# Packed attention and a channel mixer on one core: two loads placed later in the text, and the second batch's attention spread over 39 places of the first batch's loop

## The chip, the core and the metric

The kernel runs on 1 core of one Trainium2 chip. The metric is the device time of one execution in microseconds, so less is better. A core has five instruction queues that run beside each other and wait for one another through semaphores: TensorE (PE, matrix products), VectorE (DVE), ScalarE (ACT), GpSimd (POOL) and SyncE (SP, which issues the DMA transfers here). The profile lists TensorE's loading of stationary operands as a row of its own (PEld). Instructions on one queue run in the order in which the program put them there.

## The reference

There are 8 batches, 8 heads, 576 tokens, a head size of 64 and 32 "packing" queries per head. Attention runs twice, and its result goes through a token mixer of rank 32 and a channel mixer:

```python
p_packed = sm_attn(p, k, v)                  # 32 packed rows for each head
x = sm_attn(q, p_packed, p_packed)           # every token attends to those 32 rows
x = x.transpose(0, 2, 1, 3).reshape(B, S, H * D)
u = x + (x.transpose(0, 2, 1) @ U @ V).transpose(0, 2, 1)
out = u + maximum(u @ w_ch1, 0.0) @ w_ch2    # 512 -> 2048 -> 512
```

q, k, v and p are float32; U, V and both weights arrive as float64, read as pairs of 32-bit words, and are turned into float32 on the chip. `sm_attn` is a softmax over scaled scores.

## The kernel before

**Two stages.** In the first stage (up to about 121 us in the trace) 16 units, two for each batch, compute the packed rows, and the first batch's second attention is computed beside them. A scheduler orders this stage: it takes the text as given and places instructions by its own estimate of time. From line 552 on (`manual_schedule`) instructions stand on their queues in the order in which the code is written.

**The second stage.** For each batch b a loop of 16 steps kt does two products. `gemm1(kt)` makes a 128-wide slice of the hidden layer (12 TensorE products for lines 86 to 88, in two halves of 320 and 256 tokens); ScalarE takes its positive part (`hh`, `hj`), and VectorE the rest that the rounding left (`hl`, line 607). `gemm2(kt - 1)` multiplies the slice of the step before by a 128-row slice of w2, in four token tiles of three products each. Every value is carried as a high and a low part, hence three products for each.

**w2 is converted on the way.** In batch 0, step kt splits slice kt+1 into its parts (ScalarE `w2h`, line 158, GpSimd `w2l`, line 159), loads slice kt+3, and converts slice kt+2 from its 64-bit form: one ScalarE operation (line 77) and four VectorE operations in a row (lines 78 to 81). I call those four **a conversion**. Later batches have none of this.

**Folds.** At kt = 2, 6, 10, 14 `fold` multiplies the packed rows into w1 for the steps that come next: 16 products on TensorE (line 368) into two PSUM banks, and then four pairs of ScalarE `wth` (line 374) and VectorE `wtl` (line 375) that empty the banks.

**Attention in steps.** `attention(b)` returns 24 small steps for the batch after the one in the loop: `load`, then 23 others. By the names that the text uses: tq00 to tq02 and tq10 to tq12 turn the queries of head group 0 and 1 (lines 219 and 229, TensorE, then ScalarE copies, lines 226 and 230); sc0 and sc1 are the scores (line 240, TensorE, then VectorE lines 272 and 273); m0 and m1 subtract the maximum (VectorE line 278, GpSimd line 279); exp is line 282; s0 and s1 divide by the sum (VectorE lines 287 to 289, GpSimd line 290); aT0 and aT1 transpose back (VectorE line 294); tok0, tok2, tok4 (lines 247 and 249, then ScalarE line 308 and VectorE line 309), mix1 (line 316) and four v steps (lines 328 to 331) mix tokens. tq11 carries group 0's exp.

**Where steps may go.** A step kt has two places, A behind gemm1 and B behind gemm2 and the conversion (at the four fold steps the fold takes B). Four leftovers of the first stage (`rest`) sit in the middle of gemm2 of kt = 1 to 4, between its second and third tile; I call that place C. Empty entries in the list keep a place free.

**The two shared banks.** Folds, leftovers, and the steps that use TensorE all draw from one pool `psT` of two PSUM banks, in turns (`bank()`, tiles `t_ps`). A bank goes to the next user when ScalarE or VectorE has read it.

## Time and profile before

| What | Value |
| --- | --- |
| Median of 3 runs | 869.55 us (869.44 to 871.65) |
| Profiled execution, own time | 869.67 us |
| Its span, first to last instruction | 867.1 us |
| TensorE busy | 829.0 us (96%) |
| VectorE busy | 391.6 us (45%) |
| ScalarE busy | 330.2 us (38%) |
| GpSimd busy | 99.3 us (11%) |
| Batch 0's loop, first product of gemm1 of kt 0 to that of batch 1 | 121.13 to 217.09 us |

The profiled execution's own time is 2.57 us above its span and 0.12 us above the median. In rows of the timeline the first number is the start in us, the second the length in us; "x4" merges four instructions; a bracket gives the engine's idle time before the row and what ended it. In a list of waits the three numbers are the sum in us, the number of waits and the longest. A window's row has the length, and then for each engine the busy time and the number of instructions.

### The profile page before, as it was taken

Reading aid. Unit: us, or ns where it says so; the run is one execution under the profiler, and the core shown is the slowest. Engines: PE = TensorE matmul, PEld = TensorE weight load, DVE = VectorE, ACT = ScalarE, POOL = GpSimd, SP = SyncE. Lnnn points to the kernel's source line nnn. Section 1 sums busy time; section 2 is a strip of 40 time slices with the busy share of each in tenths; the row PEclk is TensorE's granted clock in tenths of the full one; section 3 lists DMA queues with packets and bytes.
Section 4 is the critical chain, followed back from the end, with each engine's and each line's share of the span. In section 5 each row is a group of like instructions: output and inputs, shape, how many; then the busy total and the mean of one; then the engine's idle time right before and its main releaser. Section 6 shows DMA issues by size and latency. Waiting matters only on the chain.

```text
span 867.1 us, 14707 instructions
## 1 busy us (share of the span) xinstructions
PE 829.0 (96%) x5792; PEld 659.4 (76%) x5792; DVE 391.6 (45%) x968; ACT 330.2 (38%) x1028; POOL 99.3 (11%) x128
## 2 busy tenths in 40 slices
PE   5879898989999999999999999999999999999997
PEld 2545566768888888788878878888888887888886
DVE  4689857797434423433343433434344234332221
ACT  3657664444432333234323333234323332342221
POOL 0002232333001100100010000110011001010000
PEclk8789999999999999999999999999999999999999
DMA  8999842332100110011001100011001100010001
GB/s 275 276 319 295 277 150 81 104 98 86 50 1 1 61 55 8 1 61 49 2 1 61 49 13 2 1 61 50 1 1 61 53 9 1 1 50 1 1 1 61
DMA packets 38981, 59.09 MB, mean 68 GB/s; under 512 B 11776, under 2 KB 21888, under 8 KB 38912
## 3 DMA queue, kind: packets, MB, share of 16 engines
q1 hardware_dynamic: 38912, 58.16, 21.1%
q8 instruction: 45, 0.74, 0.4%
q14 instruction: 24, 0.20, 0.1%
HBM read 47.79 MB, written 10.35 MB: 67 GB/s over the span
## 4 chain that ended last, share of the span: by engine, by line
PE 82%; DVE 8%; DMA 6%; ACT 2%; issue 1%; SPq 0%; POOL 0%; DVEq 0%; ACTq 0%
PE o L86 16%; PE o L88 16%; PE o L87 15%; PE h_ps L86 8%; PE h_ps L88 7%; PE h_ps L87 7%; PE t_ps L368 4%; DMA bits<-in_moe_w_ch_dram 2%; PE t_ps L219 2%; DVE os L80 1%; PE t_ps L240 1%; DVE os L78 1%; DMA kx<-in_k_dram 1%; PE s_ps L240 1%; PE t_ps L247 1%
## 5 line engine op out<-in xcount | busy, mean ns | idle before, releaser
L86 PE MATMUL o<-w2h,hh 128*128 128x512 f32 x512 | 206.4, 403 | 0.0
L88 PE MATMUL o<-w2h,hl 128*128 128x512 f32 x512 | 202.7, 396 | 0.0
L87 PE MATMUL o<-w2l,hh 128*128 128x512 f32 x512 | 202.3, 395 | 0.0
L607 DVE SCALAR_TENSOR_TENSOR hl<-h_ps,hh 128x256 fp32r<-128x256 f32 x256 | 104.3, 422 | 201.1 <-ACT hj L606 188.7
L604 ACT ACTIVATE hh<-h_ps 128x256 fp32r<-128x256 f32 x256 | 98.8, 388 | 181.2 <-PE h_ps L88 180.4
L86 PE MATMUL h_ps<-ah,wth 128*128 128x320 f32 (+1 forms) x512 | 158.0, 309 | 2.1 <-DVE hl L607 2.1
L87 PE MATMUL h_ps<-al,wth 128*128 128x320 f32 (+1 forms) x512 | 151.8, 296 | 0.0
L88 PE MATMUL h_ps<-ah,wtl 128*128 128x320 f32 (+1 forms) x512 | 151.6, 296 | 0.0
L86 PEld LDWEIGHTS h_ps<-ah,wth 128*128 128x128 f32 x512 | 96.9, 189 | 35.9 <-issue 27.0
L88 PEld LDWEIGHTS o<-w2h,hl 128*128 128x128 f32 x512 | 96.6, 189 | 22.8
L86 PEld LDWEIGHTS o<-w2h,hh 128*128 128x128 f32 x512 | 96.9, 189 | 20.0 <-issue 3.1
L87 PEld LDWEIGHTS o<-w2l,hh 128*128 128x128 f32 x512 | 96.9, 189 | 17.0
L87 PEld LDWEIGHTS h_ps<-al,wth 128*128 128x128 f32 x512 | 96.9, 189 | 1.7
L88 PEld LDWEIGHTS h_ps<-ah,wtl 128*128 128x128 f32 x512 | 97.1, 190 | 0.0
L375 DVE TENSOR_TENSOR wtl<-t_ps,wth 128x256 fp32r<-128x256 f32 x128 | 48.5, 420 | 92.5 <-ACT wth L374 89.1
L374 ACT CAST wth<-t_ps 128x256 fp32r<-128x256 f32 x128 | 43.5, 374 | 110.0 <-PE t_ps L368 95.7
L331 POOL TENSOR_TENSOR al<-aT,ah 128x320 fp32r<-128x320 f32 (+1 forms) x32 | 26.7, 836 | 206.5 <-ACT ah L330 206.5
L279 POOL TENSOR_TENSOR e<-e,m 128x576 f32<-128x576 f32 x16 | 19.7, 1229 | 236.6 <-DVE m L278 236.6
L368 PE MATMUL t_ps<-w1t,ppT 64*32 64x512 f32 x512 | 38.1, 601 | 0.3 <-DVE eT L455 0.2
L226 ACT COPY xT<-t_ps 128x256 f32<-128x256 f32 x60 | 20.4, 395 | 38.8 <-PE t_ps L219 38.2
L330 ACT CAST ah<-aT 128x320 fp32r<-128x320 f32 (+1 forms) x32 | 13.8, 434 | 46.5 <-DVE aT L329 46.5
L290 POOL TENSOR_TENSOR e<-e,s 128x576 f32<-128x576 f32 x16 | 18.6, 1160 | 106.2 <-DVE s L289 103.6
(130 smaller groups left out, 1009.6 us busy)
## 6 DMA issues: line engine op xcount, KB each, us to landing
bits<-in_moe_w_ch_dram SPq DMA_DIRECT2D x32, 512.0 KB, 4.8
kx<-in_k_dram SPq DMA_DIRECT2D x16, 576.0 KB, 6.5
x<-in_q_dram SPq DMA_DIRECT2D x16, 576.0 KB, 4.7
vt<-in_v_dram SPq DMA_DIRECT2D x64, 128.0 KB, 4.6
out_dram<-bits SPq DMA_DIRECT2D x32, 256.0 KB, 2.4
pn<-in_p_dram SPq DMA_DIRECT2D x16, 64.0 KB, 6.1
vt<-in_v_dram SPq DMA_DIRECT2D x16, 64.0 KB, 3.8
out_dram<-os SPq DMA_DIRECT2D x8, 128.0 KB, 2.3
```

Of the source, the lines that this page charges most:

```text
L86: nc.tensor.matmul(ps, lhsT=lh, rhs=rh, start=start, stop=False)
L87: nc.tensor.matmul(ps, lhsT=lh, rhs=rl, start=False, stop=False)
L88: nc.tensor.matmul(ps, lhsT=ll, rhs=rh, start=False, stop=stop)
L226: nc.scalar.copy(dst, src[:, a])
L279: nc.gpsimd.tensor_tensor(e, e, m.unsqueeze(2).to_broadcast([P, S // 32, 32]), op=ALU.subtract)
L290: nc.gpsimd.tensor_tensor(e, e, s.unsqueeze(2).to_broadcast([P, S // 32, 32]), op=ALU.mult)
L331: nc.gpsimd.tensor_tensor(al[:, g, ns], aT[:, ns], ah[:, g, ns].bitcast(F32), op=ALU.subtract)
L368: nc.tensor.matmul(f_ps[g][xs], lhsT=ppT[b][zs, g, xs], rhs=w1t[h // 2][zs, QW * c:QW * c + QW], start=True, stop=True)
L374: nc.scalar.copy(hi[:, g], f_ps[g][:, cs])
L375: nc.vector.tensor_tensor(lo[:, g], f_ps[g][:, cs], hi[:, g].bitcast(F32), op=ALU.subtract)
L604: nc.scalar.activation(hh[:, ms], src, AF.Relu)
L607: nc.vector.scalar_tensor_tensor(hl[:, ms], src, 0.0, hh[:, ms].bitcast(F32), op0=ALU.max, op1=ALU.subtract)
```

## The change

1. In the first stage the text puts the loads of w2's first two pieces and of batch 1's queries one or two units later (from units 12 and 13 to unit 14).
2. Batch 1's attention, spread over batch 0's loop, may now use C at every kt from 1 to 15 (the leftovers still take the first four). That makes 39 places, and the list of 23 steps gets 15 empty entries instead of 4; four of them come first.
3. Batch 2's `load` moves from kt 13 to kt 15 of batch 0. In batch 1 kt 0 holds no step, and place A at kt 2, 6, 10, 14 may hold one, so that batch 1's steps start one kt later and end one kt earlier. From batch 2 on nothing is changed.

```diff
-        if i == 12:
+        if i == 13:
+            fold(0, 0)
+        if i == 14:
             load_w2(0)
             load_w2(1)
-        if i == 13:
-            fold(0, 0)
             steps = attention(1, res)
             steps.pop(0)()
-        if i == 14:
             split_w2(*convert_w2(0))
             load_w2(2)
...
-    for n in (16, 15, 15, 12):
-        steps.insert(n - 1, lambda: None)
+    for n in (20, 19, 18, 15, 15, 14, 13, 12, 12, 11, 5, 0, 0, 0, 0):
+        steps.insert(n, lambda: None)
...
-            if steps and (b == 0 or kt % 4 != 2):
+            if steps and (b < 2 or kt % 4 != 2) and (b, kt) != (1, 0):
                 steps.pop(0)()
...
-                cur.gemm2(kt - 1, rest.pop(0) if rest else None)
+                cur.gemm2(kt - 1, (rest or steps).pop(0) if b == 0 and (rest or steps) else None)
...
-            elif steps:
+            elif steps and (b, kt) != (1, 0):
                 steps.pop(0)()
...
-            if ahead and kt == 13:
+            if ahead and kt == (13 if b else NK - 1):
                 ahead.pop(0)()
```

Popping both lists gives these places in batch 0 ("-" is empty; leftovers in C of kt 1 to 4 and folds in B are the same in both):

| kt | before A, B | after A, C, B |
| --- | --- | --- |
| 0 | tq00, tq01 | -, none, - |
| 1 | tq02, sc0 | -, leftover, - |
| 2 | m0, fold | tq00, leftover, fold |
| 3 | tq10, tq11 | tq01, leftover, tq02 |
| 4 | tq12, s0 | sc0, leftover, m0 |
| 5 | aT0, sc1 | -, tq10, tq11 |
| 6 | -, fold | tq12, s0, fold |
| 7 | m1, exp1 | aT0, sc1, - |
| 8 | s1, - | m1, -, - |
| 9 | -, aT1 | exp1, -, s1 |
| 10 | -, fold | -, aT1, fold |
| 11 | tok0, tok2 | -, -, tok0 |
| 12 | tok4, mix1 | tok2, tok4, - |
| 13 | v00, v10 | mix1, -, v00 |
| 14 | v01, fold | -, v10, fold |
| 15 | v11 | v01, v11 |

On the queues the first part leaves no trace: SP's queue has the same 118 rows with the same waits in both kernels, and the other queues are alike up to the first gemm1 of batch 0. What moves is in the loops of batch 0 and batch 1.

VectorE around kt 2 of batch 0, before: the end of slice 3's conversion (L80, L81), sc0's two rows (L272, L273), the residual's blocks, gemm1's `hl`, m0 (L278), a leftover (L455 to L458).

```order
L80 SCALAR_TENSOR_TENSOR os<-bits,os 128x512
L81 SCALAR_TENSOR_TENSOR os<-bits,os 128x512
L272 STREAM_TRANSPOSE e<-t_ps 128x320
L273 STREAM_TRANSPOSE e<-t_ps 128x256
L586 TENSOR_TENSOR rdl_1880<-ppall,rdh_1878 32x64 x8
L589 CAST ajl_1884<-al 128x2x64
L607 SCALAR_TENSOR_TENSOR hl<-h_ps_2061,hh 128x256
L607 SCALAR_TENSOR_TENSOR hl<-h_ps_2071,hh 128x256
L278 TENSOR_REDUCE m<-e 128x18
L455 COPY eT<-t_ps 64x128
L457 SCALAR_TENSOR_TENSOR rs<-sm 128x1
L458 RECIPROCAL rs<-rs 128x1
```

The same place of the changed kernel, whose line numbers are one lower from here on:

```order
L80 SCALAR_TENSOR_TENSOR os<-bits,os 128x512
L81 SCALAR_TENSOR_TENSOR os<-bits,os 128x512
L585 TENSOR_TENSOR rdl_1880<-ppall,rdh_1878 32x64 x8
L588 CAST ajl_1884<-al 128x2x64
L606 SCALAR_TENSOR_TENSOR hl<-h_ps_2029,hh 128x256
L606 SCALAR_TENSOR_TENSOR hl<-h_ps_2039,hh 128x256
L455 COPY eT<-t_ps 64x128
L457 SCALAR_TENSOR_TENSOR rs<-sm 128x1
L458 RECIPROCAL rs<-rs 128x1
```

sc0's and m0's three rows are gone from ahead of the leftover and of the conversion and the `wtl` rows that come next.

VectorE from kt 6 to kt 7 of batch 0 in the changed kernel: s0's last two rows, slice 8's conversion, the fold's `wtl`, `hl` of kt 7, aT0 (L294), sc1 (L272, L273).

```order
L288 TENSOR_SCALAR s<-s 128x18
L289 RECIPROCAL s<-s 128x18
L78 TENSOR_SCALAR os<-os 128x512
L79 TENSOR_SCALAR os<-os 128x512
L80 SCALAR_TENSOR_TENSOR os<-bits,os 128x512
L81 SCALAR_TENSOR_TENSOR os<-bits,os 128x512
L375 TENSOR_TENSOR wtl<-t_ps,wth 128x256 x4
L606 SCALAR_TENSOR_TENSOR hl<-h_ps_2430,hh 128x256
L606 SCALAR_TENSOR_TENSOR hl<-h_ps_2440,hh 128x256
L294 STREAM_TRANSPOSE aT_2449<-e 128x576
L272 STREAM_TRANSPOSE e<-t_ps 128x320
L273 STREAM_TRANSPOSE e<-t_ps 128x256
```

Before, s0, aT0 and sc1 were done by the end of kt 5, and neither s0's rows nor those of sc1 stood next to this fold.

TensorE at kt 12 of batch 0 in the changed kernel: tok2 (L247), the first two tiles of gemm2, tok4 (L249).

```order
L247 MATMUL t_ps<-ident,aT_2449 128x128
L247 MATMUL t_ps<-ident,aT_2611 128x128
L86 MATMUL o<-w2h_2310,hh 128x512
L87 MATMUL o<-w2l_2311,hh 128x512
L88 MATMUL o<-w2h_2310,hl 128x512
L249 MATMUL t_ps<-ident,aT_2449 64x128
L249 MATMUL t_ps<-ident,aT_2611 64x128
```

Here each kind of row stands once (four L247 and two tiles of three rows are in the queue). tok2 and tok4 are half a gemm2 apart now, and tok0 and tok2 a gemm1; before, tok0 and tok2 had a whole gemm2 between them, and tok2 and tok4 a gemm1.

## The prediction, made before the result was known

> **What bounds the kernel now.** I read the page's busy times first (in the table above), then the windows, then the list of waits inside batch 0, and last the timeline around each wait.

> ```profile
> 120.00:210.00 90.00, 82.74 (x629) 66.31 (x625) 68.76 (x131) 43.24 (x123) 27.22 (x31) 1.00 0.30 95
> 208.00:300.00 92.00, 91.63 (x588) 73.89 (x586) 36.51 (x91) 33.43 (x108) 11.29 (x13) 1.00 0.07 27
> ```

> TensorE sets the time. From batch 1 on it is hardly idle (0.37 of 92 us in the last row), so nothing is to be had there. Batch 0 leaves 7.26 us of 90 idle, and only there is VectorE close to full (68.76 of 90). The first stage is idle too, but its queues and waits are the same in both kernels. So the question is batch 0's loop, with batch 1's for a possible loss. Batch 0's waits, the three largest sorts of five:

> ```profile
> PE t_ps L219 <- DVE wtl L375: 2.7, 1, 2.7
> PE h_ps L86 <- DVE hl L607: 2.1, 3, 1.2
> PE t_ps L247 <- DVE wtl L375: 2.0, 1, 2.0
> ```

> These are 6.8 of the 7.26 us, and all three wait for VectorE. Recorded idle time is too small a measure, since the modelled tail of a product covers the start of a wait. I count instead from one start to the next. Here are the waits in order of place:

> ```profile
> 122.83 0.60 PE L219 MATMUL t_ps<-ident,x 128*128 128x128 f32 x4
> 123.60 0.66 PE L219 MATMUL t_ps<-ident,x 128*128 128x128 f32 x4 [0.17 <-ACT ppTa L481]
> 124.46 0.42 PE L86 MATMUL h_ps<-ah,wth 128*128 128x320 f32 x1 [0.21 <-DVE hl L607]
> ...
> 136.17 1.06 PE L368 MATMUL t_ps<-w1t,ppT 64*32 64x512 f32 x8
> ...
> 138.45 0.41 PE L86 MATMUL h_ps<-ah,wth 128*128 128x320 f32 x1
> ...
> 143.04 0.63 PE L219 MATMUL t_ps<-ident,x 128*128 128x128 f32 x4 [2.72 <-DVE wtl L375]
> 143.42 0.48 PE L86 MATMUL o<-w2h,hh 128*128 128x512 f32 x1
> ...
> 176.16 0.42 PE L86 MATMUL h_ps<-ah,wth 128*128 128x320 f32 x1 [0.74 <-DVE hl L607]
> ...
> 182.00 0.41 PE L86 MATMUL h_ps<-ah,wth 128*128 128x320 f32 x1 [1.19 <-DVE hl L607]
> ...
> 186.60 1.09 PE L368 MATMUL t_ps<-w1t,ppT 64*32 64x512 f32 x16
> 187.62 0.41 PE L86 MATMUL h_ps<-ah,wth 128*128 128x320 f32 x1
> ...
> 191.47 0.63 PE L247 MATMUL t_ps<-ident,aT 128*128 128x128 f32 x4 [2.00 <-DVE wtl L375]
> ...
> 210.28 2.22 PE L368 MATMUL t_ps<-w1t,ppT 64*32 64x512 f32 x16
> 212.43 0.41 PE L86 MATMUL h_ps<-ah,wth 128*128 128x320 f32 x1
> ```

> A turn (L219 x4) takes 0.38 (143.04 to 143.42), so kt 0 with two turns in 1.63 loses 0.9. A fold without a wait takes 1.02 (186.60 to 187.62); that of kt 2 takes 2.28, losing 1.26, and that of kt 14 takes 2.15, losing 1.13. The four large brackets are each short by about 0.17 of tail: 2.9, 0.9, 1.35, 2.15. **Sum before: 10.6 us.**

> **The change part by part.** *The two loads*: on the queues nothing moves, so 0. If a semaphore that the listing doesn't show differed, the first stage could shift by one load; the recorded waits for w1's and w2's bits there were the one kind touched, and I hold that at nothing. *Batch 2's load behind kt 15*: its two rows keep their place on SP, where they wait for mix1, and batch 2's queries are first used a whole gemm1 and gemm2 after kt 15. Nothing is queued behind them but the next packed rows and the first stores, with some 10 us to spare: 0.

> *The empty places at kt 0.* gemm1(1) needs VectorE's `hl`, which hangs on ScalarE:

> ```profile
> 123.28 0.27 ACT L481 COPY ppTa<-t_ps 128x128 f32<-128x128 f32 x1 [1.07 <-DMA ppTd<-ppTa]
> ...
> 123.98 0.76 DVE L607 SCALAR_TENSOR_TENSOR hl<-h_ps,hh 128x256 fp32r<-128x256 f32 x2 [3.20 <-ACT hj L606]
> ```

> ScalarE waits there for a transfer of the first stage, so gemm1(1) starts at 124.46 in either kernel. The two turns that filled part of that time now come later. The wait is the whole 122.83 to 124.46, **1.63** in place of 0.9.

> *kt 2 and 3.* VectorE before, and a plain conversion and a crowded one for comparison (first row to the row behind it):

> ```profile
> 133.49 0.51 DVE L272 STREAM_TRANSPOSE e<-t_ps 128x320 f32<-128x320 f32 x1
> ...
> 134.25 1.41 DVE L586 TENSOR_TENSOR rdl<-ppall,rdh 32x64 fp32r<-32x64 f32 x8
> ...
> 136.47 0.74 DVE L278 TENSOR_REDUCE m<-e 128x18 f32<-128x576 f32 x1
> 137.13 0.27 DVE L455 COPY eT<-t_ps 64x128 f32<-64x128 f32 x1
> ...
> 137.59 1.21 DVE L78 TENSOR_SCALAR os<-os 128x512 f32<-128x512 f32 x1
> ...
> 141.61 1.61 DVE L375 TENSOR_TENSOR wtl<-t_ps,wth 128x256 fp32r<-128x256 f32 x4
> ...
> 165.81 0.97 DVE L78 TENSOR_SCALAR os<-os 128x512 f32<-128x512 f32 x1
> ...
> 168.68 0.42 DVE L375 TENSOR_TENSOR wtl<-t_ps,wth 128x256 fp32r<-128x256 f32 x1
> ...
> 177.75 1.16 POOL L290 TENSOR_TENSOR e<-e,s 128x576 f32<-128x576 f32 x1 [3.26 <-DVE s L289]
> 178.87 1.47 POOL L159 TENSOR_TENSOR w2l<-os,w2h 128x512 fp32r<-128x512 f32 x1
> ...
> 176.35 0.74 DVE L287 TENSOR_REDUCE s<-e 128x18 f32<-128x576 f32 x1
> ...
> 177.52 0.36 DVE L78 TENSOR_SCALAR os<-os 128x512 f32<-128x512 f32 x1
> 177.92 1.28 DVE L79 TENSOR_SCALAR os<-os 128x512 int32<-128x512 int32 x1
> 179.23 1.66 DVE L80 SCALAR_TENSOR_TENSOR os<-bits,os 128x512 int32<-128x512 int32 x1
> ...
> 181.53 0.75 DVE L607 SCALAR_TENSOR_TENSOR hl<-h_ps,hh 128x256 fp32r<-128x256 f32 x2
> ```

> A conversion beside one GpSimd operation takes 2.87 (165.81 to 168.68). Beside two, w2l and a softmax operation, it takes 4.01 (177.52 to 181.53), or 4.02 (137.59 to 141.61). At kt 2 sc0 (0.76, 133.49 to 134.25) and m0 (0.66, 136.47 to 137.13) leave VectorE, and m0's GpSimd operation leaves with them, another 1.15. So `wtl` starts 2.57 earlier, at 139.0, and the fold no longer waits. TensorE arrives earlier too: sc0 (0.69 and two changes of 0.1) and tq02 (0.2) are gone, tq00 (0.45) has come, the fold's 1.26 is saved: gemm1(3) ends at 138.4 where it ended at 140.15. The bank comes back 1.43 after the first `wtl` starts (143.04 less 141.61), at 140.4. tq01 waits **1.95**, where tq10 waited 2.9, and the fold 0 for 1.26.

> *kt 4 to 6.* sc0 and m0 now stand beside one plain conversion each and no fold; adding up the rows, each `hl` is ready 1 us or more ahead of its use. No wait.

> *kt 6 and 7.* The walk brings `hl` of kt 6 to its end at 162.4 and TensorE to the fold at 163.4. s0's three rows take 1.17 (176.35 to 177.52) and stand directly ahead of slice 8's conversion, as s1 did at 177.5, so this takes 4.0. `wtl` starts near 167.5. The first bank is back 1.43 later, the second one `wtl` (0.4) after it, at 169.3. TensorE does the fold (1.1), gemm1(7) (1.7, as in 121.13 to 122.83) and two tiles of gemm2 (1.4, from 259.06 to 260.54 below, less a change) and asks for both banks for sc1 at 167.7. **1.6**. With a plain conversion it would be 0.5.

> [...]

> *kt 8 to 10.* The 0.9 and 1.35 before came of two crowded conversions in a row, with m1 and s1 at kt 7 and 8. Now m1 crowds one conversion only, and s1 stands behind one, with two empty places ahead. Each `hl` is ready 1 us or more ahead: **0**.

> *kt 11 and 12.* aT1 (0.7) goes ahead of one more conversion, but the whole gemm2 lies between the fold's `wtl` and tok0: **0.1** where it was 2.15. tok4 in place C of kt 12 needs tok0's bank, whose VectorE row stands behind a conversion that ends at 195.1: TensorE asks at 194.5 and gets it at 195.9, **1.3**.

> *kt 13 to 15.* v10 moves half a gemm2 ahead of the fold, which then finds both banks read: **0** for 1.13.

> **Sum after: 1.63 + 1.95 + 1.6 + 0.1 + 1.3 = 6.6**, 4.0 less than before. *Batch 1* gives some back: sc0 now comes directly behind a fold at kt 3, as sc1 does at kt 7 already:

> ```profile
> 257.67 0.28 PE L88 MATMUL h_ps<-ah,wtl 128*128 128x256 f32 x1
> 258.03 1.09 PE L240 MATMUL t_ps<-xT,ppT 64*32 64x320 f32 x16
> 259.06 0.50 PE L86 MATMUL o<-w2h,hh 128*128 128x512 f32 x1
> ...
> 260.54 0.39 PE L86 MATMUL o<-w2h,hh 128*128 128x512 f32 x1
> ```

> That takes 1.27 (257.79 to 259.06) for 0.8, so 0.4 lost. Two turns that stood together now stand apart, one more change of 0.1. Net gain 3.5: **869.67 - 3.5 = 866.2 us** for the profiled execution, and the median differs from that by 0.12.

> The unknown costs are the three new waits for a bank. Below, each could be nothing where VectorE runs a conversion earlier than my walk (then 4.85 more is gained); above, each could be as long as the longest wait for a bank in the trace, 2.9 (then 3.85 is lost). I take the walk's values, since each is a sum of recorded lengths, and walking the kernel before in this way came out within about 1 us at the end of batch 0.

> **Rivals.** *The waits only move.* VectorE's work in batch 0 is the same, and 68.76 of 90 us is already mean load with bursts. If sc1 waits 2.0, tok0 1.0, tok4 1.3 and the fold of kt 14 still 1.1 beside kt 0 and kt 3, the sum is 9.0, and with batch 1's 0.5 the gain is 1.1: 868.6. For it speaks that three of the waits were folds, and that folds stay. Against it, that the crowded conversions go from four to two or three.

> *Almost all waits go.* If the conversions behind m1 and s0 lose nothing, sc1 waits 0.5 and tok4 0.3: sum 4.5, gain 5.6, 864.1. Against it stands 4.01 at the same pattern.

> *Slower.* A wait in place C stops TensorE in the middle of gemm2, and five steps sit in C with a bank to take (tq10, sc1, tok4, v10, v11). If each waits 2.4 (the mean of 2.72 and 2.00), the sum is 12 + 1.63 + 1.95 = 15.6, 5.0 more than before, with batch 1 875.1. It decides from 1.4 each. Against it: tq10 takes a bank that ScalarE empties, and v10 and v11 come when conversions have ended.

> **How the numbers follow.** Forecast 0.55, waits only move 0.25, almost all go 0.14, slower 0.06. The range goes from 864.5 (short of the third) to 869.3 (past the second). A measurement of this kernel can tell about 0.3% or 2.6 us from no change, that is a time below 866.9. Of the forecast's 0.55 I put 0.46 beyond that: faster 0.60, same 0.34, slower 0.06.

> **What would show it.** Right: TensorE starts gemm1(1) at 124.46 with 1.6 us of wait; tq01 waits about 2 us for `wtl` at 140; sc1 and tok4 wait in the middle of gemm2; the two `hl` waits of 176 and 182 are gone; the windows from batch 2 on are as before. Wrong: a first stage that ends at another time, new waits for `hl`, a wait at tq10 or the v steps, or batch 1 longer by over 1 us.

## The result and the profile after

The changed kernel takes 866.91 us (median of 22 executions; 863.66 to 872.33), the kernel before 871.0 us on the same chip (22 executions). The ratio is **0.9949, with a 95% interval of [0.9931, 0.9968]**: 4.4 us less, between 2.8 and 6.0. A second comparison of the same two kernels gave 0.9963 [0.9941, 0.9985]. The forecast was 866.2 us.

The profiled execution of the changed kernel has a span of 862.9 us and an own time of 865.46 us, 4.21 less than before. Split by place, the first stage ends 0.99 earlier (the first product of gemm1(0) starts at 120.14 in place of 121.13), batch 0's loop takes 92.81 in place of 95.96, batch 1's 85.88 in place of 85.90, and the rest 564.09 in place of 564.15. So nearly all that the change itself did lies in batch 0, 3.15 us, of which 0.19 is a shorter kt 0.

The windows of the changed kernel that answer to the two shown of before, and one over the later batches, behind which the last row is that of the kernel before (length, then busy time and number of instructions of PE, PEld, DVE, ACT and POOL, then TensorE's granted clock and the transfers):

```profile
120.00:210.00 90.00, 84.16 (x619) 67.63 (x619) 69.02 (x135) 46.12 (x132) 28.24 (x28) 1.00 0.29 93
208.00:300.00 92.00, 91.67 (x583) 75.93 (x584) 37.06 (x93) 33.26 (x109) 11.39 (x14) 1.00 0.08 27
300.00:860.00 560.00, 556.90 (x3441) 459.32 (x3440) 197.13 (x490) 181.50 (x580) 42.19 (x50) 1.00 0.07 25
300.00:860.00 560.00, 558.63 (x3451) 461.45 (x3452) 200.41 (x498) 182.87 (x586) 42.88 (x51) 1.00 0.07 25
```

TensorE's idle time in the first row fell from 7.26 to 5.84 us. The row of batch 1 has 0.33 idle, where it had 0.37. Over the later batches the changed kernel's row has 1.73 us less of TensorE's work and ten products fewer, but no wait is recorded there in either kernel and the rest takes as long as before (564.09 for 564.15), so I take the later batches as unchanged. The list of TensorE's waits in batch 0, complete:

```profile
PE t_ps L240 <- DVE wtl L375: 1.7, 1, 1.7
PE t_ps L219 <- DVE wtl L375: 1.7, 1, 1.7
PE h_ps L86 <- DVE hl L606: 1.3, 1, 1.3
PE t_ps L249 <- DVE x L309: 0.8, 1, 0.8
PE t_ps L247 <- DVE wtl L375: 0.2, 1, 0.2
```

Before, the list was led by 2.7 at tq10, 2.1 in three waits for `hl`, and 2.0 at tok0. Now it is sc1 (L240), tq01 (L219), `hl` of kt 0, tok4 (L249) and a rest of tok0's. No wait is as long as 2 us. TensorE's timeline at those places:

```profile
123.28 0.42 PE L86 MATMUL h_ps<-ah,wth 128*128 128x320 f32 x1 [1.28 <-DVE hl L606]
...
134.30 1.45 PE L368 MATMUL t_ps<-w1t,ppT 64*32 64x512 f32 x16
135.68 0.42 PE L86 MATMUL h_ps<-ah,wth 128*128 128x320 f32 x1
...
139.24 0.63 PE L219 MATMUL t_ps<-ident,x 128*128 128x128 f32 x4 [1.70 <-DVE wtl L375]
...
165.39 0.40 PE L86 MATMUL o<-w2h,hh 128*128 128x512 f32 x1
167.99 1.09 PE L240 MATMUL t_ps<-xT,ppT 64*32 64x320 f32 x16 [1.74 <-DVE wtl L375]
169.01 0.50 PE L86 MATMUL o<-w2h,hh 128*128 128x512 f32 x1
...
188.58 0.40 PE L86 MATMUL o<-w2h,hh 128*128 128x512 f32 x1
189.61 0.63 PE L247 MATMUL t_ps<-ident,aT 128*128 128x128 f32 x4 [0.16 <-DVE wtl L375]
190.25 0.42 PE L86 MATMUL h_ps<-ah,wth 128*128 128x320 f32 x1
...
193.11 0.39 PE L86 MATMUL o<-w2h,hh 128*128 128x512 f32 x1
194.81 0.41 PE L249 MATMUL t_ps<-ident,aT 128*64 128x128 f32 x2 [0.84 <-DVE x L309]
...
206.86 1.09 PE L368 MATMUL t_ps<-w1t,ppT 64*32 64x512 f32 x16
207.88 0.41 PE L86 MATMUL h_ps<-ah,wth 128*128 128x320 f32 x1
```

From start to start, with 1.70 for a gemm1 and 0.70 for a tile of gemm2 (167.99 less 165.39 and less 0.70 is sc1's wait): kt 0 1.44, the fold of kt 2 0.36 (1.38 for 1.02), tq01 1.86, sc1 1.9, tok0 0.33 and 0.26 more in its own products, tok4 1.0. The fold of kt 14 is down to 1.02, and the two waits for `hl` at kt 8 and 9 are gone. VectorE ahead of sc1:

```profile
162.54 0.36 DVE L78 TENSOR_SCALAR os<-os 128x512 f32<-128x512 f32 x1
163.01 1.20 DVE L79 TENSOR_SCALAR os<-os 128x512 int32<-128x512 int32 x1
164.25 1.67 DVE L80 SCALAR_TENSOR_TENSOR os<-bits,os 128x512 int32<-128x512 int32 x1
165.95 0.69 DVE L81 SCALAR_TENSOR_TENSOR os<-bits,os 128x512 int32<-128x512 int32 x1
166.56 1.61 DVE L375 TENSOR_TENSOR wtl<-t_ps,wth 128x256 fp32r<-128x256 f32 x4
```

The conversion behind s0 took 4.02 (162.54 to 166.56), as the crowded ones of before.

### The profile page after: what moved, and what is told of

Same layout as the page of the kernel before. It is cut to its first block, busy times and chain, and to the rows that moved or that the text cites. A ratio compares the mean times of both kernels' runs of the same rounds, so it can differ in the third digit from the quotient of the medians.

```text
span 862.9 us, 14712 instructions
## 1 busy us (share of the span) xinstructions
PE 824.0 (95%) x5792; PEld 657.3 (76%) x5792; DVE 389.8 (45%) x968; ACT 330.2 (38%) x1028; POOL 99.8 (12%) x128
## 4 chain that ended last, share of the span: by engine, by line
PE 84%; DVE 8%; DMA 3%; ACT 1%; issue 1%; SPq 1%; POOL 0%; DVEq 0%; ACTq 0%; POOLq 0%
PE o L86 16%; PE o L88 16%; PE o L87 16%; PE h_ps L86 8%; PE h_ps L88 7%; PE h_ps L87 7%; PE t_ps L368 3%; DVE os L80 2%; DMA bits<-in_moe_w_ch_dram 2%; PE t_ps L240 1%; PE t_ps L219 1%; PE t_ps L316 1%; PE s_ps L240 1%; DVE os L78 1%; DMA x<-in_moe_U_dram 1%
## 5 line engine op out<-in xcount | busy, mean ns | idle before, releaser
L86 PE MATMUL o<-w2h,hh 128*128 128x512 f32 x512 | 206.8, 404 | 0.0
L88 PE MATMUL o<-w2h,hl 128*128 128x512 f32 x512 | 202.5, 396 | 0.0
L606 DVE SCALAR_TENSOR_TENSOR hl<-h_ps,hh 128x256 fp32r<-128x256 f32 x256 | 104.0, 422 | 202.2 <-ACT hj L605 190.2
L86 PE MATMUL h_ps<-ah,wth 128*128 128x320 f32 (+1 forms) x512 | 157.3, 307 | 1.3 <-DVE hl L606 1.3
L88 PE MATMUL h_ps<-ah,wtl 128*128 128x320 f32 (+1 forms) x512 | 151.4, 296 | 0.0
L86 PEld LDWEIGHTS h_ps<-ah,wth 128*128 128x128 f32 x512 | 96.8, 189 | 32.9 <-issue 26.0
L88 PEld LDWEIGHTS o<-w2h,hl 128*128 128x128 f32 x512 | 96.5, 188 | 22.8
L86 PEld LDWEIGHTS o<-w2h,hh 128*128 128x128 f32 x512 | 96.8, 189 | 21.4 <-issue 4.6
L88 PEld LDWEIGHTS h_ps<-ah,wtl 128*128 128x128 f32 x512 | 97.0, 189 | 0.0
L375 DVE TENSOR_TENSOR wtl<-t_ps,wth 128x256 fp32r<-128x256 f32 x128 | 48.5, 419 | 91.2 <-ACT wth L374 87.9
L368 PE MATMUL t_ps<-w1t,ppT 64*32 64x512 f32 x512 | 36.3, 601 | 0.0
L290 POOL TENSOR_TENSOR e<-e,s 128x576 f32<-128x576 f32 x16 | 18.6, 1160 | 107.0 <-DVE s L289 104.4
```

The source lines that it names most:

```text
L86: nc.tensor.matmul(ps, lhsT=lh, rhs=rh, start=start, stop=False)
L88: nc.tensor.matmul(ps, lhsT=ll, rhs=rh, start=False, stop=stop)
L290: nc.gpsimd.tensor_tensor(e, e, s.unsqueeze(2).to_broadcast([P, S // 32, 32]), op=ALU.mult)
L368: nc.tensor.matmul(f_ps[g][xs], lhsT=ppT[b][zs, g, xs], rhs=w1t[h // 2][zs, QW * c:QW * c + QW], start=True, stop=True)
L375: nc.vector.tensor_tensor(lo[:, g], f_ps[g][:, cs], hi[:, g].bitcast(F32), op=ALU.subtract)
L606: nc.vector.scalar_tensor_tensor(hl[:, ms], src, 0.0, hh[:, ms].bitcast(F32), op0=ALU.max, op1=ALU.subtract)
```

## The experiments

A single time mixes in where the first stage happens to end: over the two profiles so far and the ten of the next five subsections, all with the same queues in that stage, the first product of gemm1(0) starts anywhere from 118.14 to 122.27. kt 0 also varies, from 2.96 to 3.95, with a transfer that ScalarE waits for (1.07 idle ahead of line 481 in the trace before). I therefore compare batch 0's loop **from kt 1 on**, from the first product of gemm1(1) to that of batch 1: 92.63 us before, 89.67 after.

A fall of TensorE's clock to half, which some of the profiles show in batch 0's loop and neither of the first two does there, is named where it occurs, and taken up in the last sections.

### The parts of the change one by one

The two loads alone, on the kernel before:

```diff
-        if i == 12:
+        if i == 13:
+            fold(0, 0)
+        if i == 14:
             load_w2(0)
             load_w2(1)
-        if i == 13:
-            fold(0, 0)
             steps = attention(1, res)
             steps.pop(0)()
-        if i == 14:
             split_w2(*convert_w2(0))
```

> The kernel before with the first part of the change alone: w2's first loads and the second batch's load stand at unit 14 in the text. The queues are those of the kernel before, row by row. My theory: nothing moves; batch 0's loop (first product of its gemm1 to that of batch 1's) stays 95.96 us and the rest behind it 650.0 us, ratio 1.000. Rival (the loads' part made the first stage end 0.99 us earlier in the changed kernel's profile): the first gemm1 starts about 1 us earlier than 121.13 and the ratio is about 0.999; if the first stage's length is luck of the run, it lies within 2 us on either side.

Measured: 871.23 us, a ratio of 1.0013 [0.9992, 1.0033]. The loop from kt 1 on is 94.19, of which 1.56 is a fall of the clock at kt 11, and 92.63 without it. The loads alone bring no gain that shows, as forecast. The rival asked for a first product about 1 us earlier than 121.13, and in this profile it is at 120.13. But with the loads at their old place (the next run) it is at 119.66, and over the ten profiles with the new place it goes from 118.14 to 122.27, so one profile can't show such a shift, and the ratio doesn't: the rival's 0.999 lies just outside the interval.

Batch 1's places and batch 2's load alone, on the kernel before:

```diff
-            if steps and (b == 0 or kt % 4 != 2):
+            if steps and (b < 2 or kt % 4 != 2) and (b, kt) != (1, 0):
...
-            elif steps:
+            elif steps and (b, kt) != (1, 0):
...
-            if ahead and kt == 13:
+            if ahead and kt == (13 if b else NK - 1):
```

> The kernel before with the third part alone: batch 1's steps start one kt later and may use place A at the fold steps, batch 2's load stands at kt 15. My theory: batch 0's loop 95.96 us as before. Batch 1's loop 85.9 us: sc0 behind the fold of kt 3 loses 0.4 to 0.5 us, and kt 15 without v11 behind the fold of kt 14 wins about 0.4. Rival (this part brings some of the gain): batch 1's loop shorter than 85.90 by over 0.5 us, or batch 0's shorter than 95.96.

Measured: batch 0 from kt 1 on 92.64, batch 1 85.90, as before. One time, 868.46, which its loops don't explain and its first stage does (the first product at 119.66). So what the change does, it does in batch 0's places.

### Which of the places

The changed kernel with the steps up to tq11 at their old places, and then with all steps up to aT1 there, so that only tok0 to v11 stand as in the change:

```diff
-    for n in (20, 19, 18, 15, 15, 14, 13, 12, 12, 11, 5, 0, 0, 0, 0):
+    for n in (7, 8, 9, 10, 11, 16, 18, 19, 21, 23, 25, 26, 30, 32, 34):       # x5_front
+    for n in (10, 12, 13, 15, 18, 19, 20, 21, 23, 24, 25, 26, 30, 32, 34):    # x6_back
```

> The changed kernel with the steps up to tq11 at the places that they had before (tq00 and tq01 at kt 0, tq02 and sc0 at kt 1, m0 at kt 2, tq10 and tq11 at kt 3); from tq12 on as changed. My theory (each place has its own wait): kt 0 to 3 lose 5.1 us again in place of 3.7, the later waits are as in the changed kernel, so batch 0's loop takes 92.81 + 1.4 = 94.2 us. Rival (the work of VectorE sets the whole loop's length and the waits only move): within 0.5 of 92.8.

> The changed kernel with all steps up to aT1 at the places that they had before; from tok0 on as changed. My theory: waits as before up to kt 10 (0.9, 1.26, 2.9, 0.9, 1.35 us) and as changed from kt 11 on (0.6 at tok0, 1.0 at tok4, none at the fold of kt 14, 0.25 at v01), 9.2 in all: batch 0's loop 95.96 - 1.4 = 94.5 us. Rival (waits only move): tok0 or the fold of kt 14 keep their old waits and the loop takes 95.5 us or more.

Measured: 870.76 and 866.06 us (one execution each). Both have the old wait of 2.72 at tq10, and in both the clock fell behind it, for 1.49 and 1.43 us. Without that, the loop from kt 1 on is 90.41 and 90.38. Read as steps from 92.63 down to 89.67: the places of tok0 to v11 give 2.25 us, those of tq12 to aT1 give nothing, and those of tq00 to tq11 give 0.74. In the middle piece one sort of wait was traded for another: with the old places two waits for `hl` (0.73 and 1.19 recorded) stand, with the new ones sc1 waits 1.36 and tok4 0.33 longer. The forecasts for the whole loop, 94.2 and 94.5, came out at 94.1 and 93.7 without the fall. The first is a hit by luck. By the waits that it was counted from, kt 0 was to take 0.5 less than in the changed kernel's profile and the loop from kt 1 on 1.9 more; kt 0 took 0.57 more (3.71) and the rest 0.74 more. In the second the places of tok0 to v11 gave 2.25 where 1.4 had been counted.

### Moving one step at a time

tq00 and tq01 to kt 0 (x1), sc1 from place C to B of kt 7 (x2), tok4 from place C to B of kt 12 (x3), each alone on the changed kernel:

```diff
-    for n in (20, 19, 18, 15, 15, 14, 13, 12, 12, 11, 5, 0, 0, 0, 0):
+    for n in (2, 3, 4, 5, 9, 16, 18, 19, 21, 23, 25, 26, 30, 32, 34):         # x1_fill
+    for n in (0, 1, 2, 3, 9, 15, 18, 19, 21, 23, 25, 26, 30, 32, 34):         # x2_sc1
+    for n in (0, 1, 2, 3, 9, 16, 18, 19, 21, 23, 25, 26, 29, 32, 34):         # x3_tok4
```

> The changed kernel with tq00 and tq01 back at kt 0 (places A and B), so that place A of kt 2 and kt 3 is empty. My theory: kt 0 loses 0.7 to 0.9 us in place of 1.44; no step asks for a bank in place A of kt 3, so the 1.86 there goes, and the leftover in place C, half a gemm2 later, waits 0.5 at most. Batch 0's loop 92.81 - 2.1 = 90.7 us. Rival (waits only move): the same wait comes up at the leftover or at the next hl, loop 92.3 us or more.

> The changed kernel with sc1 in place B of kt 7 in place of C, half a gemm2 and a conversion later; nothing else moves. My theory: both banks are back by then, the 1.9 us wait for wtl and the slow sc1 behind it go (2.15 together), at most 0.3 comes back. Batch 0's loop 92.81 - 1.9 = 90.9 us. Rival (waits only move): m1's rows or an hl wait as long, loop 92.3 us or more.

> The changed kernel with tok4 in place B of kt 12 in place of C. My theory: the 1.0 us wait for tok0's bank goes, loop 91.8 us; mix1 still finds its inputs. Rival (waits only move): mix1 or tok4 waits as long, loop 92.5 us or more.

Measured: 863.92, 864.44 and 866.43 us (one execution each). *x1* lost the wait of kt 3 as expected: kt 3 takes 8.67 in place of 10.99, and kt 4 to 6 are as they were, so it doesn't come back there. The whole loop, 92.36, is by its number the rival's (92.3 or more). Two things hide the gain in it: kt 0 took 3.70, and the clock fell behind sc1's wait, which made kt 7 1.13 and kt 8 0.44 longer, and tok0's wait at kt 11 0.27 shorter. From kt 1 on the loop is 88.66, and 87.36 without the fall, 2.3 less than in the changed kernel. The part of the forecast for kt 0, 0.7 to 0.9 lost, missed: 1.24 was lost. *x2* and *x3* missed. TensorE's waits from kt 7 to kt 11 with sc1 in B:

```profile
166.54 1.09 PE L240 MATMUL t_ps<-xT,ppT 64*32 64x320 f32 x16 [0.34 <-DVE wtl L375]
...
177.53 0.42 PE L86 MATMUL h_ps<-ah,wth 128*128 128x320 f32 x1 [0.72 <-DVE hl L606]
...
188.56 0.63 PE L247 MATMUL t_ps<-ident,aT 128*128 128x128 f32 x4 [0.77 <-DVE wtl L375]
```

and the one that replaced tok4's with tok4 in B:

```profile
199.80 0.35 PE L316 MATMUL t_ps<-x,ua 128*128 128x256 f32 x1 [0.75 <-DVE x L309]
```

With sc1 in B, kt 7 is 1.50 shorter, and kt 8 to 11 are 0.19, 1.00, 0.09 and 0.62 longer: the loop from kt 1 on is 90.08, 0.41 more than in the changed kernel. With tok4 in B, kt 12 is 1.11 shorter and kt 13 1.05 longer, since mix1 needs what tok4's VectorE row makes: 89.61. VectorE is the engine that is late from kt 6 to kt 13, and each of the two steps of TensorE that were moved behind their own wait there only carried TensorE to VectorE's next late row.

### Taking VectorE's delay away

```diff
-            nc.gpsimd.tensor_tensor(e, e, s.unsqueeze(2).to_broadcast([P, S // 32, 32]), op=ALU.mult)
+            if (b, g) != (1, 0):
+                nc.gpsimd.tensor_tensor(e, e, s.unsqueeze(2).to_broadcast([P, S // 32, 32]), op=ALU.mult)
```

> The changed kernel without GpSimd's multiplication by 1/sum for batch 1's head group 0 (that part of the softmax is left out, so its rows stay undivided). The order and all other work stay. My theory (two GpSimd operations beside one conversion make it 4.0 us long): the conversion ahead of the fold's wtl at kt 6 takes 2.9 us in place of 4.02, wtl starts 1.1 earlier and sc1's wait at kt 7 shrinks from 1.9 to about 0.8: batch 0's loop 91.6 us. Rival (the conversion's length hangs on its own operands or on ScalarE, not on that GpSimd operation): conversion still 4.0, loop 92.8 us.

Measured: 865.41 us (one execution), the loop 91.83 (forecast 91.6), and 88.56 from kt 1 on, 1.11 less than in the changed kernel. sc1's row with that operation left out (lines count one higher in this kernel):

```profile
168.12 1.09 PE L240 MATMUL t_ps<-xT,ppT 64*32 64x320 f32 x16 [0.51 <-DVE wtl L376]
```

The wait falls from 1.74 to 0.51. VectorE and GpSimd ahead of it:

```profile
162.89 1.29 POOL L159 TENSOR_TENSOR w2l<-os,w2h 128x512 fp32r<-128x512 f32 x1 [3.01 <-ACT w2h L158]
163.51 0.69 DVE L288 TENSOR_SCALAR s<-s 128x18 f32<-128x18 f32 x1
164.42 0.36 DVE L78 TENSOR_SCALAR os<-os 128x512 f32<-128x512 f32 x1
166.69 1.61 DVE L376 TENSOR_TENSOR wtl<-t_ps,wth 128x256 fp32r<-128x256 f32 x4
```

The conversion takes 2.27 (164.42 to 166.69), where 2.9 was expected. With the multiplication gone, `w2l` ran earlier too, beside s0's second row, which took 0.69 in place of 0.18, and the conversion had no GpSimd operation beside it at all. s0's three rows and the conversion together take 3.95 in place of 5.19. Here VectorE is earlier, and what was gained at sc1 is kept. This is the price of GpSimd's multiplication ahead of the fold, shown by taking it away: 1.1 to 1.2 us.

### All places set anew

If VectorE's order, and not TensorE's, makes the waits, then the steps have to be spread by what they put on VectorE. y_all does that with the same 39 places; tq00 and tq01 stand at kt 0, as in x1, tq02 at kt 1, sc0 and m0 about half a step earlier than in the change, the steps from sc1 to mix1 one place to a whole step later, so that s1 and aT1 don't crowd the same conversion and tok0 stands further behind the fold of kt 10. The changed kernel itself ran beside it, its list only written in another order.

```diff
-    for n in (20, 19, 18, 15, 15, 14, 13, 12, 12, 11, 5, 0, 0, 0, 0):
+    for n in (0, 1, 2, 3, 9, 16, 18, 19, 21, 23, 25, 26, 30, 32, 34):         # after_same
+    for n in (2, 4, 5, 9, 10, 14, 16, 17, 20, 21, 22, 25, 27, 29, 32):        # y_all
```

> The changed kernel again, its list of empty places written in ascending order and nothing else altered, timed on the same chip as the kernel before and as the next one. Theory (the gain comes from the first two batches): batch 0's loop, from the first product of its first multiplication to that of batch 1, 92.8 us as in the profile after, waits (start to start) of 7.7 us in it, and 0.995 of the time before. Rival (the gain seen so far owes something to the chip it was taken on): a ratio at or above 0.998.

> The changed kernel with the 15 empty places moved, so that all steps stand otherwise: tq00 to A0 and tq01 to B0 (the wait of kt 0 gets a product group more to be filled with), sc0 and m0 at B3 and A4, tq10, tq11 and tq12 at B4, B5 and A6, s0 and aT0 at C6 and C7, and from the fold of kt 6 on the attention's steps spread so that none of the TensorE ones stands directly behind a fold. Theory 1 (a wait at a step is set by what VectorE has before it at that step, and a place clear of the folds takes it away): counted row by row from the durations of the profile after, kt 0 keeps 0.9 us, a step at kt 3 0.4, the product behind the hl of gemm1(12) 1.3 and others some 0.4, so 3.0 in place of 7.7; batch 0's loop 92.8 - 4.7 = 88.1 us, the time 4.5 us under the changed kernel's. Theory 2 (VectorE is behind over the whole stretch from kt 5 to kt 12, as the runs that moved one step suggest, and waits that leave one place appear at the next): two thirds of what is taken at the old places comes back, the loop stays at or above 91.2 us, and the time is within 1.6 us of the changed kernel's.

Measured: the changed kernel 866.75 us, 0.9963 [0.9941, 0.9985] of before, its loop from kt 1 on 89.67 again (the whole loop 93.32, with 3.65 for kt 0). y_all 863.76 us, **0.992 [0.9889, 0.995]** of before. Its loop is 88.91 us, where 88.1 was counted ahead of the run and the rival said 91.2 or more; from kt 1 on it is 85.67, 4.0 under the changed kernel. Of these, 2.3 lie in kt 1 to 5 (31.59 for 33.93), as much as x1 gave there with tq00 and tq01 alone (31.62); the other 1.6 lie from kt 6 on (54.09 for 55.73), where VectorE's work was spread anew. No run tells apart which of the moves from kt 6 on brought them. The window over the loop and the complete waits in it:

```profile
122.00:210.00 88.00, 86.16 (x622) 69.03 (x622) 71.59 (x138) 46.75 (x134) 28.95 (x28) 1.00 0.29 94
```

```profile
125.01 0.41 PE L86 MATMUL h_ps<-ah,wth 128*128 128x320 f32 x1 [0.21 <-DVE hl L606]
...
188.22 0.42 PE L86 MATMUL h_ps<-ah,wth 128*128 128x320 f32 x1 [1.19 <-DVE hl L606]
```

The one long wait is that for the `hl` of gemm1(12), where 1.3 had been counted. TensorE idles 1.84 of 88 us, and VectorE is busy for 71.59 of them: the mean load that the rival of the prediction took for a bound was no bound in this order, whose steps were placed so that VectorE's bursts stand apart. The medians differ by 3.0 us and the two intervals overlap a little; that y_all is the fastest of the three is shown by the traces, and its lead over the changed kernel by the times only roughly.

### TensorE's clock behind a wait

In four of the profiles (e1_loads, x5_front, x6_back, x1_fill; the text below counts three) the granted clock fell to 0.50 behind a wait of batch 0's loop, and in others not, at the same wait (behind the 2.72 at tq10 in x5_front and x6_back, not in the kernel before). Graded waits, in batches where there are none otherwise:

```diff
         def fold(b, c):
...
+        if 1 <= b <= 6 and c in (2, 3):
+            for _ in range((2 + (b - 1 + 3 * (c - 2)) % 6)):
+                nc.vector.tensor_reduce(scratch, f_ps[0], axis=AX.X, op=ALU.max)
```

> The changed kernel with 2 to 7 maximum reductions more on VectorE in the folds of kt 6 and kt 10 of batches 1 to 6, ahead of the operation that the next use of the bank waits for: waits of TensorE of twelve graded lengths, from about 1.5 to 5 us. They add nothing to what is computed. Theory 1 (the granted clock falls to 0.50 for some 3.4 us behind a long wait of TensorE): the falls of the clock stand behind these waits and nowhere else, behind all of the waits of over 3.4 us and some of those of 1.7 to 3.4, and each costs the products behind it 1.1 to 1.5 us beside the wait. Theory 2 (the falls in three of the ten profiles so far came from something else and stood behind waits by chance): no more than one or two falls, at places that have nothing to do with the length of the waits.

Measured: twelve waits, two each of 1.59, 2.32, 3.04, 3.77, 4.49 and 5.22 us. Ten were followed by a fall, the two of 1.59 were not, and no fall stood anywhere else from batch 1 on. Theory 1 holds. What had not been expected is their form: all ten last 3.41 or 6.83 us, and their starts differ by whole multiples of 3.413 us (283.98, 365.90, 389.79, 461.47, ... are 24, 7, 21 cells apart). So the windows can be laid on that grid. Three of the waits (1.59 at 258.47, 3.77 at 280.95, 5.22 at 485.21), cell by cell:

```profile
256.67:260.09 3.42, 1.83 (x15) 1.65 (x14) 2.73 (x6) 1.64 (x7) 0.00 (x0) 1.00 0.00 0
260.09:263.50 3.41, 3.41 (x27) 2.28 (x28) 2.50 (x6) 0.39 (x2) 0.49 (x1) 1.00 0.02 5
...
280.57:283.98 3.41, 0.38 (x4) 0.17 (x2) 2.82 (x6) 0.89 (x3) 0.00 (x0) 1.00 0.00 0
283.98:287.39 3.41, 2.67 (x8) 2.18 (x9) 1.97 (x6) 1.51 (x6) 0.00 (x0) 0.50 0.00 0
...
485.37:488.78 3.41, 0.00 (x0) 0.00 (x0) 3.00 (x5) 0.19 (x1) 0.00 (x0) 1.00 0.00 0
488.78:492.19 3.41, 1.76 (x7) 1.60 (x8) 2.26 (x7) 2.43 (x8) 0.00 (x0) 0.50 0.02 5
492.19:495.61 3.42, 3.42 (x10) 2.65 (x9) 0.67 (x1) 0.00 (x0) 0.00 (x0) 0.50 0.00 0
```

The clock is 1.00 or 0.50 through each of these cells, and what TensorE did in one cell goes with the clock of the next. Why five of the ten falls lasted a second cell is open. The last run tried that rule ahead of time, with twelve waits of one length:

```diff
-            for _ in range((2 + (b - 1 + 3 * (c - 2)) % 6)):
+            for _ in range(3):
```

> The changed kernel with three more maximum reductions on VectorE in each of the folds of kt 6 and kt 10 of batches 1 to 6: twelve waits of TensorE of one length, 2.3 us. They add nothing to what is computed. In the profiles so far all falls of the clock begin on a grid of 3.413 us that runs through the whole execution, and last one or two of its cells. Theory 1 (the grid cell decides): the granted clock is 0.50 in a cell if in the cell before it TensorE spent more than about 2.35 of the 3.413 us without the products of lines 86 to 88, idle or in the small products of the other lines (over the profiles so far the largest such time without a fall is 2.29, the smallest with one 2.38). By that, waits of one length behave differently: some 4 to 8 of the 12 fall, and each falls or not as its own cell says. Theory 2 (the length of the wait decides): the two waits of 2.32 us with a fall behind both speak for all 12 falling, or, with the waits of 2.72 us that had none, for falls that no cell explains.

Measured: all waits 2.3 us; 10 of 12 were followed by a fall, where 4 to 8 were expected, all ten starting on one grid. Two without a fall and one with, each with the cell behind:

```profile
250.11:253.53 3.42, 2.09 (x20) 1.66 (x12) 2.52 (x5) 0.65 (x2) 0.00 (x0) 1.00 0.00 0
253.53:256.94 3.41, 2.42 (x22) 1.53 (x23) 3.02 (x8) 1.38 (x5) 0.00 (x0) 1.00 0.02 5
...
274.01:277.42 3.41, 1.39 (x11) 1.18 (x9) 2.74 (x6) 1.32 (x5) 0.00 (x0) 1.00 0.00 0
277.42:280.83 3.41, 3.11 (x9) 2.52 (x10) 1.64 (x5) 1.07 (x5) 0.00 (x0) 0.50 0.00 0
...
646.06:649.47 3.41, 1.92 (x20) 1.66 (x12) 2.68 (x5) 0.80 (x3) 0.00 (x0) 1.00 0.00 0
649.47:652.89 3.42, 2.60 (x23) 1.66 (x24) 3.03 (x8) 1.23 (x5) 0.00 (x0) 1.00 0.03 7
```

The grid holds: waits of one length behaved differently, and the two without a fall are the two that a border cut nearest to the middle, into 1.33 and 0.99, and into 1.49 and 0.82. The amount that I had put on it failed: four of the falls follow cells with 1.99 to 2.25 us, short of 2.35, outside the products of lines 86 to 88.

## Why the prediction was right, and where its terms were off

| Term of the sum | before | forecast | measured after |
| --- | --- | --- | --- |
| `hl` at kt 0 | 0.9 | 1.63 | 1.44 |
| fold of kt 2 | 1.26 | 0 | 0.36 |
| kt 3 (tq10, now tq01) | 2.9 | 1.95 | 1.86 |
| sc1 at kt 7 | 0 | 1.6 | 1.9, and 0.2 in its products |
| `hl` at kt 8 and 9 | 0.9 + 1.35 | 0 | 0 |
| tok0 | 2.15 | 0.1 | 0.6 |
| tok4 | 0 | 1.3 | 1.0 |
| fold of kt 14 | 1.13 | 0 | 0 |
| sum over batch 0 | 10.6 | 6.6 | 7.4 |
| batch 1 | 0 | +0.5 | 0 |

**The forecast case came about.** Each wait that the prediction removed is gone, but for 0.36 at the fold of kt 2, and each that it added is there, at its place and for its reason. Batch 0 gained 3.15 where 4.0 was forecast, batch 1 lost nothing where 0.5 was forecast, so the change's own part is 3.2 in place of 3.5. That the total is nearer than its parts is luck: the two misses, 0.85 and 0.5, point opposite ways. Of the prediction's signs of being wrong one appeared, a first stage that ends at another time (0.99 us earlier); over the first twelve profiles it ends anywhere in some 4 us, so that sign told nothing of the change. The later batches take as long as before, and the loads show no gain, alone either. Of the rivals, "the waits only move" fell for the change as a whole: no tenth of a microsecond is left at kt 8, 9 and 14. "Almost all waits go" fell too: the crowded conversion at kt 6 took 4.02, as the argument against this rival had it, and sc1 and tok4 lost 2.1 and 1.0 where it put 0.5 and 0.3. "Slower" fell with it: of the five steps in C only sc1 and tok4 wait for a bank that VectorE holds.

**Terms that were mis-sized.** The waits that came are 0.8 longer than forecast. tok0 was to wait 0.1 and lost 0.6, sc1 1.6 and lost 2.1, and the fold of kt 2 nothing and lost 0.36. For sc1 the crowded conversion's length was right (4.02 for 4.0). But counted from the fold, at 163.4 in the walk and at 161.97 in the trace, the first `wtl` came 0.5 later than walked (166.56 for 166.07), and TensorE asked 0.2 earlier (166.09 for 166.27). What the walk added for the second bank, 0.4, did not come: sc1 starts 1.43 behind the first `wtl`. At kt 3 the walk's own rows bring TensorE to 138.25, not 138.4, which would have made tq01's wait 2.1 for the measured 1.86. For tok0 the walk had left out that aT1 needs GpSimd's part of s1, the step right before it. VectorE stood still for that, with the conversion, the `wtl` rows and tok0's bank behind it:

```profile
184.86 0.78 DVE L294 STREAM_TRANSPOSE aT<-e 128x576 f32<-128x576 f32 x1 [0.67 <-POOL e L290]
```

kt 0 is not a fixed term: its first product to the next takes 3.33 before, and in profiles with the old order 2.96 to 3.95, in the changed one 3.14 and 3.65, with the transfer that ScalarE waits for. What the change did is clearer from kt 1 on, 2.96 us in both profiles of the changed kernel.

**Batch 1.** sc0 behind the fold does cost what was forecast (from the end of gemm1 at 229.95 to the next tile of gemm2 at 231.23, 1.28 for 0.8). What the prediction left out is kt 15: before, v11 stood there behind the fold of kt 14 and its products took from 299.73 to 300.18, 0.45 with 0.25 of waiting. That place is now empty, since v11 stands at kt 13 (the steps end two kt earlier, not one), and kt 15 is 0.46 shorter.

**GpSimd beside the conversion.** The prediction put sc1's wait at 1.6 behind a crowded conversion and at 0.5 behind a plain one. From start to start the runs gave 1.9 with GpSimd's multiplication and 0.67 without. The traces agree: L79 takes 1.20 beside the multiplication and L80 1.67 beside `w2l` in the changed kernel, and 0.43 and 0.69 in the run without the multiplication, where no GpSimd operation runs beside them; the kernel before has the same 0.43 and 0.69 at such a place:

```profile
162.60 0.43 DVE L79 TENSOR_SCALAR os<-os 128x512 int32<-128x512 int32 x1
163.07 0.69 DVE L80 SCALAR_TENSOR_TENSOR os<-bits,os 128x512 int32<-128x512 int32 x1
```

GpSimd's `w2l` ends at 162.28 there, and its next operation starts at 165.22. What lengthens the rows beside GpSimd's, no run shows.

**What the method missed.** Terms of a sum of waits were treated as independent. For the change itself that did little harm, since it moves work of VectorE along with the steps. For single steps it failed twice: what kt 7 gained in x2, 1.50, was repaid at kt 8 to 11 with 1.90, and what kt 12 gained in x3, 1.11, at kt 13 with 1.05, the next places where TensorE met VectorE late. It was not repaid where VectorE had caught up by then (x1, 2.32 less at kt 3, and no wait of TensorE recorded from 123.34 to 165.74), was relieved (x4, 1.11 kept) or had its work respread (y_all, 1.6 less from kt 6 on).

**How the profiles' gain fits the measured one.** The pair of profiles gives 3.2 us for the two loops, and 4.2 with a first stage that ended earlier; the comparisons gave 4.4 (2.8 to 6.0) and 3.2. The 3.2 of the loops lies in both intervals, so a further gain isn't shown. Falls of the clock may add one that neither of the two profiles has in its loops. Over all profiles that have them, the old wait of 2.72 at tq10 was followed by a fall in 2 of 5 and the old wait of 2.0 at tok0 in 1 of 3; sc1's wait of 1.74 in 1 of 6. With the mean price of the four falls, 1.5 us, that is an estimated 1.1 us per execution before and 0.25 after. So few profiles can't show it, and the first stage's luck is larger.

## What to carry to other kernels

Where two engines alternate in being late, find the one whose work sets the pace of the stretch, and spread what the steps put on that engine; moving a step of the waiting engine behind its wait carried the wait to the next meeting point twice here, and paid off only where the late engine had caught up before the next one. A high mean load (81% of VectorE in y_all) did not bound the stretch: TensorE idled 1.84 of 88 us there. Look for pieces of work that take longer beside each other, here a conversion beside GpSimd's operations (4.02 us in the changed kernel, 2.27 in x4 with none beside it), and place them apart. When single profiles of one kernel disagree by a microsecond or two, as a fall of the clock (1.43 to 1.57 us here) can make them, lay TensorE's clock beside its waits before any difference is put down to an edit.

## What the hardware showed that was not expected

```profile
138.78:142.19 3.41, 1.53 (x12) 1.33 (x10) 2.89 (x6) 0.31 (x2) 1.18 (x1) 1.00 0.01 2
142.19:145.60 3.41, 2.56 (x46) 1.96 (x47) 1.66 (x5) 1.92 (x7) 0.00 (x0) 1.00 0.46 161
```

```profile
187.98:191.39 3.41, 1.42 (x10) 1.17 (x9) 2.92 (x8) 1.99 (x7) 0.00 (x0) 1.00 0.38 124
191.39:194.80 3.41, 3.41 (x10) 2.63 (x9) 2.85 (x4) 1.08 (x2) 1.28 (x1) 0.50 0.08 30
```

Before, a border of the grid cut the wait of 2.72 into 1.88 and 0.85, and nothing followed; in the other kernel a wait of 1.99 lay whole in a cell of the grid, and the next cell ran at half the clock. A fall cost 1.56, 1.49, 1.43 and 1.57 us in the four profiles, beside the wait itself (the last in kt 7 and 8 of x1, with 0.27 saved later). The one fall behind less idling:

```profile
163.49:166.90 3.41, 1.67 (x20) 0.56 (x19) 3.27 (x9) 2.14 (x7) 0.18 (x1) 1.00 0.36 95
166.90:170.31 3.41, 3.41 (x10) 2.84 (x11) 3.20 (x7) 0.32 (x1) 1.11 (x1) 0.50 0.15 59
```

That cell (x1) has 1.74 idle and sixteen of sc1's small products (64 by 32) besides. Whether those count as half idle is open; no run told it apart.
